# First group's attention in one fixed instruction order, with its value sums and key copies on GpSimd

## The chip, the cores and the metric

The kernel runs on one core of a Trainium2 chip. The metric is the device time of one execution in microseconds (us). A core has five engines that run their own instruction streams and wait for each other by semaphores: TensorE (PE in the profile; PEld is its weight loading), VectorE (DVE), ScalarE (ACT), GpSimd (POOL) and SyncE (SP), which here issues most of the DMAs.

## What is computed

Three layers run one behind the other on 8 x 576 = 4608 tokens of width 512, all in float32:

```python
# attention: q, k, v are (8, 8, 576, 64); keys and values averaged over 8 neighbours
k_p = k.reshape(B, H, Sp, pool, D).mean(axis=3)          # Sp = 72
v_p = v.reshape(B, H, Sp, pool, D).mean(axis=3)
attn = softmax(scale * q @ k_p.T);  x = attn @ v_p       # -> (4608, 512)
# first MLP: w_in (512, 2048), w_out (2048, 512)
h = x @ w_in;  g = max(h, 0) + log1p(exp(-abs(h)));  x = g @ w_out
# second layer: tokens with x @ w_skip > 0 go to the best of 8 experts (512 -> 1024 -> 512)
out = x + gate * (relu(x @ w1[e]) @ w2[e])               # other tokens: out = x
```

## The kernel before

Tokens are worked off in nine groups of 512 (G). For each group the attention makes x for four head pairs; a head pair with its tokens is a **unit**, and x is kept in two parts, `xh` (rounded to the matmul's own float32 format) and `xl` (the rest). The first MLP then goes through 16 chunks c of 128 hidden columns: `p1(g, c)` is 12 matmuls of 512 columns into `h` (L716), a softplus of four ScalarE and two VectorE instructions (Abs L722, Exp L723, Ln L724, the sum L725, the rounded part `gh` L727, the rest `gl` L729), and `p2(g, c)`, two chunks later, is 12 matmuls into four banks `y` (L740 to L742). p1 of a chunk reads the first half of that chunk's weight tile, and p2 of chunk c reads the second half of tile c + 2.

The weights arrive as raw words and are converted on the way, during group 0: two ScalarE instructions on the raw words (`unpack`, L470 and L472), two on VectorE (`join`, L475 and L477), the rounded part `wh` on ScalarE (L492 or L520) and the rest `wl` on VectorE (L494 or L521). `load_weights` is a generator with one such step per `next`; chunks 0 to 3 (`EARLY`) go by halves of 512 elements (L470 to L494, `half`), chunks 4 to 15 by pairs of 2 x 1024 (L520, L521).

Group 0's units (`unit0`) pool the keys on VectorE (`kp`, L531), copy them into a block-diagonal tile `kbd` on ScalarE (L538, L539), make the scores `s` on TensorE (L586), the maximum and the subtraction on VectorE (L594, L595), the exponential on ScalarE (L543), its sum, an addition and the reciprocal on VectorE (L544 to L546) and the multiplication on GpSimd (L547). The values are summed over 8 neighbours and turned in one go by 8 matmuls with the identity (L604), the shares are turned by transposes (`tr`, L613) and copied by ScalarE (`et`, L614), and two pairs of matmuls make the output `o` (L570), from which come `xh` (ScalarE, L572) and `xl` (VectorE, L573). Units of later groups (`unit`) sum their values on VectorE (L554).

Each engine's order is made when the program is built, by a scheduler that goes by priorities (program order, and 250 places ahead for group 0's softplus); instructions of the first units, of the conversions and of group 1's first units are therefore interleaved. SyncE issues the loads in the order in which the code asks for them; three raw buffers serve the six early halves.

Of the kernel before, what the change touches and what calls it, by code (L numbers as in the profile page):

```python
# [9 lines left out]
F32 = mybir.dt.float32  # L10
# [10 lines left out]
P = 128  # L21
# [4 lines left out]
SP = 72  # L26
# [10 lines left out]
def tile_kernel(ctx, tc, qT, kT, vT, wbits, w9, w1, w2, out):  # L37
# [383 lines left out]
    with ExitStack() as ph:  # L421
# [37 lines left out]
        STEPS = 6 * EARLY + 6 * (8 - EARLY // 2)  # L459
# [4 lines left out]
        def load_weights():  # L464
# [15 lines left out]
            def half(c, j, first):  # L480
# [8 lines left out]
                unpack(lo, hi)  # L489
# [10 lines left out]
            for c in range(EARLY):  # L500
                for j in range(2 if c >= LAG else 1):
                    yield from half(c, j, True)
            for i in range(EARLY // 2, 8):
# [5 lines left out]
                for j in range(2):  # L509
                    lo, hi = raw[:, j, :, 0], raw[:, j, :, 1]  # L510
                    unpack(lo, hi)
# [15 lines left out]
        count = [0]  # L527
        def keys(u, k, kv):
            if u not in pooled:
                kp = pp.tile([P, SP], F32, tag="kp", name="kp")  # L530
                nc.vector.tensor_reduce(kp, k.rearrange("p (s w) -> p s w", w=8), AX.X, ALU.add)  # L531
                v = kv()
                nc.sync.dma_start(out=v, in_=vT[u])
                pooled[u] = (kp, v, None)
# [15 lines left out]
        def sums(us, vr):  # L550
            for u, *_ in us:
                kp, v, vp = pooled[u]
                if vp is None:
                    nc.vector.tensor_reduce(vr, v.rearrange("p (s w) -> p s w", w=8), AX.X, ALU.add)  # L554
# [11 lines left out]
        def output(us, et, hp, xh, xl, ps=ps_a, tag="pa"):  # L566
            o = ps.tile([P, 512], F32, tag=tag, name="o")
# [4 lines left out]
            nc.scalar.activation(out=xh[:, hp, :], in_=o, func=AF.Copy, scale=0.125)  # L572
            nc.vector.scalar_tensor_tensor(out=xl[:, hp, :], in0=o, scalar=0.125,  # L573
                                           in1=xh[:, hp, :].bitcast(F32), op0=ALU.mult, op1=ALU.subtract)

        def unit0(hp, us, xh, xl, g):
            (u, r0, rn, c0), = us
            q, k = room("q", G, True), room("kv", 576, True)
            nc.sync.dma_start(out=k, in_=kT[u])
            nc.sync.dma_start(out=q, in_=qT[u, :, r0:r0 + rn])  # L580
            yield
            yield
            banks = [ps_y.tile([P, 512], F32, tag=f"y{hp % 2 * 2 + i}", name="s") for i in range(2)]
            kb = keys(u, k, lambda: room("kv", 576, True))
            for t in range(T):
                nc.tensor.matmul(banks[t // 3][:, t % 3 * 144:(t % 3 + 1) * 144],  # L586
                                 lhsT=q[:, t * P:(t + 1) * P], rhs=kb, start=True, stop=True)
            e = k.rearrange("p (a k) -> p a k", k=SP)
            st = room("st", 24, True)
            mx, sm, rc = (st[:, i * 8:(i + 1) * 8] for i in range(3))  # L590
            for b, (i, j) in enumerate(((0, 3), (3, 4))):
                s3 = banks[b][:, :(j - i) * 144].rearrange("p (a k) -> p a k", k=SP)
                m = mx[:, 2 * i:2 * j]
                nc.vector.tensor_reduce(m, s3, AX.X, ALU.max)  # L594
                nc.vector.tensor_tensor(out=e[:, 2 * i:2 * j], in0=s3, op=ALU.subtract,  # L595
                                        in1=m.unsqueeze(2).to_broadcast([P, 2 * (j - i), SP]))
            shares(e, sm, rc)
            yield
            yield
            kp, v, _ = pooled[u]  # L600
            v8 = v.rearrange("p (s w) -> p w s", w=8)
            pv = ps_h.tile([P, 512], F32, tag="h", name="pv")
            for w in range(8):
                nc.tensor.matmul(pv[:SP, :P], lhsT=v8[:, w], rhs=ident, start=w == 0, stop=w == 7)  # L604
            vp = pp.tile([SP, P], F32, tag="vp", name="vp")
# [411 lines left out]
```

## Time and profile before

| | us |
|---|---|
| median of 3 runs | 1362.04 (1360.51 to 1363.50) |
| the profiled execution, device time | 1360.56 |
| its span on the core | 1358.8 |
| TensorE busy in the span | 1330.1 (98%) |
| VectorE, ScalarE, GpSimd busy | 847.6, 595.0, 308.0 |

The profiled execution is 1.5 us under the median of the runs, and 1.8 us of it lie outside the span. TensorE is busy almost throughout, so the time is what TensorE has to do plus the places where it has to wait. In the 40 slices of the page (34 us each) the first slice has TensorE at six tenths; ScalarE and VectorE are at nine tenths in the two slices behind it and fall to five and seven tenths afterwards. [...]

### The profile page before, as it was taken

The numbers are of one execution on the slowest core, as the hardware profiler recorded it, in microseconds if no ns is written. First come the engines' busy times: TensorE is split into PE (matmuls) and PEld (weight loads), VectorE is DVE, ScalarE is ACT, GpSimd is POOL, SyncE is SP. The second block draws the span as 40 slices with busy tenths as digits, with TensorE's granted clock in tenths as the row PEclk, the third lists the DMA queues.
The fourth block names the chain that finished last, engine by engine and source line by source line (L and its number), as shares of the span: only waits on it lengthen the run. The fifth ranks groups of instructions, "written<-read, shape, count | busy, mean of one in ns | idle before, by whom it ended". The sixth has DMA issues, their size and how long they took to land. (4 is left out here: it accounts for less than half of the span.)

```text
span 1358.8 us, 21365 instructions
## 1 busy us (share of the span) xinstructions
PE 1330.1 (98%) x7030; PEld 1110.0 (82%) x7030; DVE 847.6 (62%) x1951; ACT 595.0 (44%) x1076; POOL 308.0 (23%) x375
## 2 busy tenths in 40 slices
PE   6999999999999999999999999999999999999996
PEld 5777787778878778778778778889989898989885
DVE  7998794974974964965946847545655332326263
ACT  6996544544555445545455444551111111114152
POOL 2010111121021030030130120343233343233334
PEclk9999999999999999999999999999999999999998
DMA  7642432241341340431421301503322222243363
GB/s 274 256 150 79 125 106 68 77 126 35 83 128 29 99 125 17 119 102 31 119 70 28 111 14 46 196 23 94 96 79 95 71 63 75 69 136 112 123 212 88
DMA packets 149743, 134.17 MB, mean 99 GB/s; under 512 B 100933, under 2 KB 116933, under 8 KB 147056
## 3 DMA queue, kind: packets, MB, share of 16 engines
q1 hardware_dynamic: 131744, 95.51, 24.3%
q0 software_dynamic: 17872, 37.13, 8.6%
q8 instruction: 60, 0.98, 0.3%
q14 instruction: 67, 0.55, 0.1%
HBM read 168.77 MB, written 29.67 MB: 146 GB/s over the span
## 5 line engine op out<-in xcount | busy, mean ns | idle before, releaser
L716 PE MATMUL h<-xh,wt 128*128 128x512 f32 x1152 | 379.7, 390 | 0.3 <-DVE xl L573 0.3
L716 PEld LDWEIGHTS h<-xh,wt 128*128 128x128 f32 x1152 | 216.2, 188 | 46.0 <-DVE xl L573 1.2
L740 PE MATMUL y<-wt,gh 128*128 128x512 f32 x576 | 232.8, 404 | 0.0
L894 PE MATMUL h<-xt,w1h 128*128 128x256 f32 x1280 | 226.4, 281 | 2.7 <-PEq L918 2.0
L120 DVE CUSTOM_DVE_ANT_0 junk<-rows,w9b 128x512 bf16<-128x512 f32 x324 | 222.4, 686 | 8.1 <-ACT rows L114 3.2
L741 PE MATMUL y<-wt,gh 128*128 128x512 f32 x576 | 225.2, 391 | 0.0
L742 PE MATMUL y<-wt,gl 128*128 128x512 f32 x576 | 225.1, 391 | 0.0
L716 PE MATMUL h<-xl,wt 128*128 128x512 f32 x576 | 224.7, 390 | 0.0
L894 PEld LDWEIGHTS h<-xt,w1h 128*128 128x128 f32 x1280 | 196.4, 188 | 5.1 <-issue 2.8
L894 PE MATMUL h<-xt,w1l 128*128 128x256 f32 x640 | 179.5, 280 | 0.7 <-DVEq L962 0.7
L898 ACT ACTIVATE hs<-h 128x512 fp32r<-128x512 f32 x80 | 47.7, 598 | 301.5 <-PE h L894 180.3
L722 ACT ACTIVATE a<-h 128x512 f32<-128x512 f32 x144 | 85.8, 596 | 175.8 <-PE h L716 169.7
L725 DVE SCALAR_TENSOR_TENSOR a<-h,a 128x512 f32<-128x512 f32 x144 | 98.5, 684 | 102.8 <-ACT a L724 102.2
L727 ACT ACTIVATE gh<-a 128x512 fp32r<-128x512 f32 x144 | 90.8, 631 | 160.6 <-DVE a L725 158.2
L740 PEld LDWEIGHTS y<-wt,gh 128*128 128x128 f32 x576 | 108.1, 188 | 35.2 <-ACT a L722 7.7
L742 PEld LDWEIGHTS y<-wt,gl 128*128 128x128 f32 x576 | 108.2, 188 | 25.5 <-issue 2.1
L716 PEld LDWEIGHTS h<-xl,wt 128*128 128x128 f32 x576 | 108.2, 188 | 22.3 <-issue 0.2
L741 PEld LDWEIGHTS y<-wt,gh 128*128 128x128 f32 x576 | 108.3, 188 | 20.0 <-issue 0.2
L729 DVE TENSOR_TENSOR gl<-a,gh 128x512 fp32r<-128x512 f32 x144 | 101.0, 701 | 37.6 <-ACT gh L727 34.9
L894 PEld LDWEIGHTS h<-xt,w1l 128*128 128x128 f32 x640 | 122.1, 191 | 0.9 <-DVEq L962 0.9
L928 DVE SCALAR_TENSOR_TENSOR ys<-y,xg 128x512 f32<-128x512 f32 x38 | 28.5, 750 | 145.3 <-PE y L926 115.8
L926 PE MATMUL y<-w2h,hs 128*128 128x512 f32 x304 | 118.5, 390 | 0.6 <-DVE hs L899 0.6
(198 smaller groups left out, 1815.0 us busy)
## 6 DMA issues: line engine op xcount, KB each, us to landing
w9b<-w SPq DMA_DIRECT2D x81, 256.0 KB
raw<-wbits SPq DMA_DIRECT2D x12, 1024.0 KB
x2d<-rows SPq DMA_DIRECT2D x36, 260.0 KB
et<-q SPq DMA_DIRECT2D x256, 32.0 KB
kv<-vT SPq DMA_DIRECT2D x28, 288.0 KB
kv<-kT SPq DMA_DIRECT2D x24, 288.0 KB
xm<-misc SPq DMA_DIRECT2D x160, 32.0 KB
misc<-misc SPq DMA_DIRECT2D x144, 32.0 KB
```

The costliest lines, as they stand in the source:

```text
L120: nc.vector.tensor_tensor_reduce(out=ws["junk"], in0=rows[t][:, :D], in1=w9b[e], scale=1.0, scalar=0.0, op0=ALU.mult, op1=ALU.add, accum_o ...
L716: nc.tensor.matmul(h, lhsT=l, rhs=r[:, kk, :], start=n == 0, stop=n == 11)
L722: nc.scalar.activation(out=a, in_=h, func=AF.Abs)
L725: nc.vector.scalar_tensor_tensor(out=a, in0=h, scalar=0.0, in1=a, op0=ALU.max, op1=ALU.add)
L727: nc.scalar.activation(out=gh, in_=a, func=AF.Copy)
L729: nc.vector.tensor_tensor(out=gl, in0=a, in1=gh.bitcast(F32), op=ALU.subtract)
L740: nc.tensor.matmul(y, lhsT=th, rhs=wh, start=c == 0, stop=False)
L741: nc.tensor.matmul(y, lhsT=th, rhs=wl, start=False, stop=False)
L742: nc.tensor.matmul(y, lhsT=tl, rhs=wh, start=False, stop=c == 15)
L894: nc.tensor.matmul(h[:, f2, :], lhsT=l, rhs=r[:, kk, :], start=n == 0, stop=n == 11)
L898: nc.scalar.activation(out=hh[:, fs, :], in_=h, func=AF.Relu)
L926: nc.tensor.matmul(y, lhsT=hl[:, f, js], rhs=ws["w2h"][:, f, :], start=False, stop=f == 7)
```

## The change

Group 0's attention is written as methods of a class `Unit0`, and a function `lead_in` calls them in one list. `in_order` then ties every instruction of an engine in that list to the one before it on the same engine, so the scheduler keeps the list's order on each engine; it may still put other instructions between.

- All four key, query and value loads are asked for first, then three raw weight halves; the later three halves follow, each two conversions ahead.
- A unit's pooled keys are copied to `kbd` by GpSimd instead of ScalarE.
- The values are summed by three GpSimd additions per unit (`add8`) and turned by one matmul, instead of 8 matmuls.
- Conversions of chunks 0 and 1 stand behind the units' exponentials. Conversions of chunks 2 and later wait for the last unit's `xh` on ScalarE, group 1's first pooling of a new batch for the last `xl` on VectorE, and the first two p1 blocks for the last transposes on TensorE (`issue_after`).

The core of the diff:

```diff
+                if first:
+                    yield
+                with after("ACT", first and c > 1):
+                    unpack(lo, hi)
...
-            for c in range(EARLY):
-                for j in range(2 if c >= LAG else 1):
-                    yield from half(c, j, True)
+            its = [half(c, j, True) for c in range(EARLY) for j in range(2 if c >= LAG else 1)]
+            for n in range(2):
+                next(its[n])
+                yield
+            for n, it in enumerate(its):
+                if n + 2 < len(its):
+                    next(its[n + 2])
+                yield from it
...
+        def add8(out, t):
+            t3 = t.rearrange("p (s w) -> p s w", w=8)
+            for n in (4, 2):
+                nc.gpsimd.tensor_tensor(out=t3[:, :, :n], in0=t3[:, :, :n], in1=t3[:, :, n:2 * n], op=ALU.add)
+            nc.gpsimd.tensor_tensor(out=out.unsqueeze(2), in0=t3[:, :, 0:1], in1=t3[:, :, 1:2], op=ALU.add)
...
+            def key(self):
...
+                nc.gpsimd.tensor_copy(self.kb[0:64, 0:SP], kp[0:64, :])
+                nc.gpsimd.tensor_copy(self.kb[64:128, SP:2 * SP], kp[64:128, :])
...
+            def vsum(self):
+                add8(self.vr, self.v)
...
+            with after("PE", g == 0 and c < 2):
...
-        feed.start(units_of(0), 1)
-        for i, it in enumerate(feed.units):
-            next(it)
-            if i:
-                weights(1)
-        while feed.units or jobs:
-            feed.tick()
+        def lead_in():
+            u0, u1, u2, u3 = us = units_of(0)
+            for u in us:
+                u.load_v()
+            weights(2)
+            u0.key()
+            u0.score()
+            u1.key()
+            u1.score()
+            u0.top()
+            u2.key()
+            u0.exp()
+            u0.share()
+            u2.score()
+            u0.vsum()
+            u1.top()
+            u1.exp()
+            u3.key()
+            u1.share()
+            u0.value()
+            u0.turned()
+            u3.score()
+            u2.top()
+            u2.exp()
+            u1.vsum()
+            u0.product()
+            u0.high()
+            u3.top()
+            u2.vsum()
+            u2.share()
+            u1.value()
+            u1.turned()
+            u3.exp()
+            u3.share()
             weights(1)
+            u1.product()
+            u1.high()
+            u3.vsum()
+            weights(1)
+            u0.low()
+            u1.low()
...
+        with in_order():
+            lead_in()
```

What stands where in the built programs, at three places. First GpSimd, behind the constants at the program's start. Before, four multiplications of group 0 (`boot_kv` holds keys, values and exponentials of group 0) are followed by group 1's (`q`):

```order
L88 CAST tok_i<-tok_f 128x36
L547 TENSOR_TENSOR boot_kv<-boot_kv,boot_171 128x576 x4
L649 MEMSET q 128x8x24
L547 TENSOR_TENSOR q<-q,st 128x8x72
L649 MEMSET q 128x8x24
```

and now, from the copies of the third unit's keys on:

```order
L637 COPY kbd_165<-kp 64x72
L638 COPY kbd_165<-kp 64x72
L662 TENSOR_TENSOR boot_kv<-boot_kv,boot_171 128x576
L612 TENSOR_TENSOR boot_kv<-boot_kv 128x72x4
L612 TENSOR_TENSOR boot_kv<-boot_kv 128x72x2
L613 TENSOR_TENSOR boot_171<-boot_kv 128x72
L637 COPY kbd_167<-kp 64x72
L638 COPY kbd_167<-kp 64x72
L662 TENSOR_TENSOR boot_kv<-boot_kv,boot_171 128x576
L612 TENSOR_TENSOR boot_kv<-boot_kv 128x72x4
L612 TENSOR_TENSOR boot_kv<-boot_kv 128x72x2
```

Copies and value sums have come between the multiplications (L662) of one unit and the next; on TensorE a unit's value matmul now stands ahead of its transposes.

Second, ScalarE at the program's start. Before, behind the first two units' key copies (`boot_171` are raw weight words, `boot_kv` an exponential):

```order
L470 ACTIVATE boot_171<-boot_171 128x512
L472 ACTIVATE boot_171<-boot_171 128x512
L543 ACTIVATE boot_kv<-boot_kv 128x576
L492 ACTIVATE wt_181<-boot_171 128x512
L470 ACTIVATE boot_171<-boot_171 128x512
L472 ACTIVATE boot_171<-boot_171 128x512
L543 ACTIVATE boot_kv<-boot_kv 128x576
```

and now, behind the table load:

```order
L655 ACTIVATE boot_kv<-boot_kv 128x576
L553 ACTIVATE kbd_165<-kp 64x72
L554 ACTIVATE kbd_165<-kp 64x72
L655 ACTIVATE boot_kv<-boot_kv 128x576
L579 ACTIVATE vp<-pv 72x128
L678 ACTIVATE boot<-tr 72x512 x2
L655 ACTIVATE boot_kv<-boot_kv 128x576
L589 ACTIVATE xh<-o 128x512
```

The exponentials (L655) have moved ahead of all conversions, and two key copies of group 1's first unit (L553, L554) have slipped in behind the first one.

Third, ScalarE ahead of the rounded weights of chunks 4 and 5 (L520 before, L529 now), in group 0's p1 blocks. Before, from the first Abs on (`raw_450` is the raw pair of chunks 4 and 5, `raw_516` of 6 and 7):

```order
L722 ACTIVATE a<-h 128x512
L472 ACTIVATE raw_450<-raw_450 128x1024
L723 ACTIVATE a<-a 128x512
L538 ACTIVATE kbd_167<-kp 64x72
L724 ACTIVATE a<-a 128x512
L722 ACTIVATE a<-h 128x512
L539 ACTIVATE kbd_167<-kp 64x72
L723 ACTIVATE a<-a 128x512
L470 ACTIVATE raw_516<-raw_516 128x1024
L727 ACTIVATE gh<-a 128x512
L724 ACTIVATE a<-a 128x512
L520 ACTIVATE wt_511<-v 128x1024 x2
```

and now, the last twelve rows ahead of the same place (`raw_504` is the pair 4 and 5, `raw_581` the pair 6 and 7, L799 the fourth chunk's Abs):

```order
L558 ACTIVATE q<-q 128x8x72
L470 ACTIVATE raw_504<-raw_504 128x1024
L799 ACTIVATE a<-h 128x512
L495 ACTIVATE wt_190<-boot_171 128x512
L800 ACTIVATE a<-a 128x512
L472 ACTIVATE raw_504<-raw_504 128x1024
L801 ACTIVATE a<-a 128x512
L470 ACTIVATE raw_581<-raw_581 128x1024
L472 ACTIVATE raw_581<-raw_581 128x1024
L804 ACTIVATE gh<-a 128x512
L470 ACTIVATE raw_581<-raw_581 128x1024
L529 ACTIVATE wt_533<-v 128x1024 x2
```

The pair's rounding stood behind 11 instructions counted from the first Abs, in the second chunk's softplus; it now stands behind 35, in the fourth chunk's, with three of the next pair's four unpackings ahead of it. From the end of group 1 on, the order of all engines is as it was.

## Rows read from the trace of the kernel before

**Rows 1.** Busy time by stage; columns: stage, length, engines' busy time, clock, DMA share, GB/s.

```profile
0.00:35.40 35.40, 24.32 (x146) 19.97 (x146) 26.12 (x55) 23.71 (x48) 8.36 (x45) 1.00 0.81 281
35.40:74.75 39.35, 37.56 (x171) 29.23 (x172) 37.35 (x49) 39.20 (x60) 2.48 (x3) 1.00 0.65 247
74.75:120.00 45.25, 45.04 (x205) 33.53 (x204) 42.51 (x57) 36.28 (x60) 4.45 (x4) 1.00 0.33 100
```

**Rows 2.** Timeline, TensorE: start, duration, line, tile; idle time before and its releaser.

```profile
35.41 0.50 PE L716 MATMUL h<-xh,wt 128*128 128x512 f32 x1 [0.32 <-DVE xl L573]
...
42.40 1.39 PE L636 MATMUL s<-kbd,q 128*64 128x144 f32 x8 [1.22 <-ACT kbd L539]
...
54.52 0.39 PE L716 MATMUL h<-xh,wt 128*128 128x512 f32 x1
...
66.20 0.39 PE L716 MATMUL h<-xh,wt 128*128 128x512 f32 x1
...
74.75 0.39 PE L716 MATMUL h<-xh,wt 128*128 128x512 f32 x1
```

**Rows 3.** Timeline, VectorE: the rests of the weights of chunks 4 to 7.

```profile
49.27 1.22 DVE L521 TENSOR_TENSOR wt<-v,wt 128x1024 fp32r<-128x1024 f32 x1
...
60.84 2.34 DVE L521 TENSOR_TENSOR wt<-v,wt 128x1024 fp32r<-128x1024 f32 x2
```

**Rows 4.** Timeline, TensorE, group 0's attention.

```profile
5.22 2.29 PE L586 MATMUL s<-kbd,boot 128*128 128x144 f32 x8 [5.22 <-ACT kbd L539]
...
16.61 2.81 PE L604 MATMUL pv<-ident,boot_kv 128*72 128x128 f32 x16
19.25 1.15 PE L586 MATMUL s<-kbd,boot 128*128 128x144 f32 x8
...
31.91 1.07 PE L613 MATMUL tr<-ident,boot_kv 128*72 128x128 f32 x8
32.91 1.08 PE L570 MATMUL o<-boot,vp 72*64 72x512 f32 x4
```

**Rows 5.** Timeline, ScalarE, group 0's attention and the early halves.

```profile
4.62 0.26 ACT L538 ACTIVATE kbd<-kp 64x72 f32<-64x72 f32 x1 [2.54 <-DVE kp L531]
...
9.66 0.66 ACT L470 ACTIVATE boot<-boot 128x512 f32<-128x512 f32 x1 [2.05 <-DMA boot<-wbits]
10.22 0.64 ACT L472 ACTIVATE boot<-boot 128x512 int32<-128x512 uint32 x1
...
28.41 1.09 ACT L614 ACTIVATE boot<-tr 72x512 f32<-72x512 f32 x2
```

**Rows 6.** Timeline, VectorE, group 0's attention: maxima, and the sum of an exponential.

```profile
7.07 0.82 DVE L594 TENSOR_REDUCE boot<-s 128x6 f32<-128x432 f32 x2
...
11.49 0.75 DVE L544 TENSOR_REDUCE boot<-boot_kv 128x8 f32<-128x576 f32 x1
```

**Rows 7.** Timeline, GpSimd: a multiplication of group 0 and one of group 1.

```profile
18.32 1.15 POOL L547 TENSOR_TENSOR boot_kv<-boot_kv,boot 128x576 f32<-128x576 f32 x1 [3.06 <-DVE boot L546]
...
51.61 1.97 POOL L547 TENSOR_TENSOR q<-q,st 128x576 f32<-128x576 f32 x1 [7.49 <-ACT a L724]
```

**Rows 8.** VectorE's early rests: all six (min/median/max), and the longest on the timeline.

```profile
L494 DVE TENSOR_TENSOR wt<-boot,wt x6: 687/692/1399, 13.6 to 38.9; 128x512 fp32r<-128x512 f32 x6
...
18.61 1.40 DVE L494 TENSOR_TENSOR wt<-boot,wt 128x512 fp32r<-128x512 f32 x1 [0.43 <-ACT wt L492]
```

**Rows 9.** Timeline, ScalarE in group 0's p1 blocks: first Abs, rounding of 4 and 5, prices.

```profile
38.73 0.63 ACT L722 ACTIVATE a<-h 128x512 f32<-128x512 f32 x1
...
45.00 1.99 ACT L520 ACTIVATE wt<-v 128x1024 fp32r<-128x1024 f32 x2
...
53.62 0.62 ACT L723 ACTIVATE a<-a 128x512 f32<-128x512 f32 x1
54.15 1.14 ACT L470 ACTIVATE raw<-raw 128x1024 f32<-128x1024 f32 x1
55.18 0.62 ACT L724 ACTIVATE a<-a 128x512 f32<-128x512 f32 x1
```

More of the change, by code (lines that the diff above doesn't have):

```diff
@@ L1 @@
 import math
-from contextlib import ExitStack
+from contextlib import ExitStack, contextmanager, nullcontext
 import concourse.bass as bass
@@ L510, in load_weights @@
                     lo, hi = raw[:, j, :, 0], raw[:, j, :, 1]
-                    unpack(lo, hi)
+                    with after("ACT", i < 4):
+                        unpack(lo, hi)
                     yield
@@ L527, in tile_kernel, with after @@
         count = [0]
+        behind = {}
+        def after(eng, cond=True):
+            return tc.issue_after(behind[eng]) if cond else nullcontext()
         def keys(u, k, kv):
@@ L530, in keys @@
                 kp = pp.tile([P, SP], F32, tag="kp", name="kp")
-                nc.vector.tensor_reduce(kp, k.rearrange("p (s w) -> p s w", w=8), AX.X, ALU.add)
+                with after("DVE", u == 4):
+                    nc.vector.tensor_reduce(kp, k.rearrange("p (s w) -> p s w", w=8), AX.X, ALU.add)
                 v = kv()
@@ new lines, in round_x, with rest_x, in_order @@
+        def round_x(o, hp, xh):
+            return nc.scalar.activation(out=xh[:, hp, :], in_=o, func=AF.Copy, scale=0.125)
+        def rest_x(o, hp, xh, xl):
+            return nc.vector.scalar_tensor_tensor(out=xl[:, hp, :], in0=o, scalar=0.125,
+                                                  in1=xh[:, hp, :].bitcast(F32), op0=ALU.mult, op1=ALU.subtract)
+        @contextmanager
+        def in_order():
+            traced = nc.cur_bb.bb.instructions
+            mark = traced[-1]
+            yield
+            start = next(k for k in reversed(range(len(traced))) if traced[k] is mark) + 1
+            prev = {}
+            for ins in traced[start:]:
+                if ins.engine in prev:
+                    tc.add_manual_dep(ins, prev[ins.engine].name,
+                                      mybir.DependencyInfo(mybir.DependencyClass.NoSync, mybir.DependencyReason.DATA),
+                                      reason="in_order")
+                prev[ins.engine] = ins
@@ L785, in last_group @@
                 split2()
-        feed.start(units_of(0), 1)
-        for i, it in enumerate(feed.units):
-            next(it)
-            if i:
-                weights(1)
-        while feed.units or jobs:
-            feed.tick()
-            weights(1)
+        def lead_in():
[32 more added lines that the diff above has]
+            u3.share()
+            weights(1)
+            u1.product()
[4 more added lines that the diff above has]
+            u1.low()
+            u2.value()
+            u2.turned()
+            weights(1)
+            u3.value()
+            u3.turned()
+            weights(1)
+            u2.product()
+            u2.high()
+            u2.low()
+            weights(1)
+            u3.product()
+            u3.high()
+            weights(1)
+            u3.low()
+        with in_order():
+            lead_in()
         pend = []
```

129 lines of the change are left out of this document (72 added, 57 removed).

## The prediction

> **What bounds the kernel now.** I read the busy time by stage first. Up to 35.4 us TensorE does group 0's attention; from 35.4 to 74.75 it is busy 37.56 of 39.35 us, from 74.75 to 120 45.04 of 45.25 [rows 1]. So time can be won in three places: the start of the first p1 matmul at 35.41, a 1.22 us wait at 42.40 and some 0.6 us of waits up to 74.75 [rows 1, 2]. The second reading is who is full beside it: from 35.4 to 74.75 ScalarE is busy 39.20 and VectorE 37.35 of 39.35 us [rows 1], with the softplus and the conversion of the weights. TensorE runs only just behind them. The rests of chunks 4 and 5 are done at 49.27 + 1.22 = 50.5 and wanted at 54.52; those of 6 and 7 at 60.84 + 2.34 = 63.2, wanted at 66.20 [rows 2, 3]: a stock of 4 and 3 us. ScalarE paid for it early: 23.71 us of work were done before 35.4 [rows 1], most of the six early halves among them (their rests run on VectorE from 13.6 on [rows 8]). An earlier start of p1 is therefore worth what this stock allows, less what the change takes out of it.
>
> **The change, part by part.** All times are estimates of one walk through the new orders, with the durations of the rows; a step on GpSimd gets 0.14 us to start behind another engine (the multiplication at 18.32 starts so behind a reciprocal [rows 7]).
>
> *Key copies on GpSimd.* ScalarE loses 8 copies of 0.26 [rows 5], 2.2 us with gaps. GpSimd shows no such copy; I take 0.25 each, ScalarE's price, and bound it by 0.1 and 0.5. Scores of the first unit start at 5.3, as before.
>
> *Value sums on GpSimd.* Removed are 64 matmuls of TensorE, 16 in 2.81 us [rows 4], some 9.5 us of work in which TensorE hid its other waits; they need no engine before them but the load. Added are 12 GpSimd additions over 288, 144 and 72 elements. The nearest row is the multiplication of 576 in 1.15 us, 1.97 beside VectorE [rows 7], so 0.6, 0.36 and 0.24 us, with handing over 1.6 us a unit (1.2 to 2.7).
>
> *The chain on GpSimd.* Unit 0's exponential starts at 9.5, no conversion being ahead of it; sum (0.75 [rows 6]), addition and reciprocal end at 11.4, multiplication at 12.8, sum of its values at 14.4. Its transposes stand behind the value matmul and go at 14.7, not 12.8. Unit 1's exponential stands on ScalarE behind group 1's two copies, which wait for unit 2's scores (10.8 + 2.29 [rows 4] = 13.1): 13.7; its reciprocal ends at 15.6, its multiplication at 17.0, the sums of values 1 and 2 at 20.2. Unit 2 is multiplied by 21.6. Unit 3's multiplication meets VectorE's joins, which read two operands: VectorE's rest of 0.69 took 1.40 in the one place where it met a multiplication (18.61 beside 18.32 [rows 7, 8]), and multiplications spread from 1.15 to 1.97. I add 0.6: 22.5 to 24.3. The last value sum ends at 25.9. [...]
>
> *From there to p1.* Value matmul, 8 transposes (1.07 [rows 4]), two copies (1.09 [rows 5]) and the last product (about 0.55) put the first p1 matmul at 28.4, 7.0 us earlier than 35.41. But the second early half has its unpack (2 x 0.56, the step from 9.66 to 10.22 [rows 5]) behind the last copies on ScalarE, its join behind that on VectorE (31.4), its rounding (32.1) ahead of the last `xh` (32.6), and `xl` ends at 33.4. So the 24 matmuls of chunks 0 and 1 wait 2.2 us inside and end at 36.4; before, at 42.40 - 1.22 = 41.2 [rows 2]. The lead is down to 4.8 us.
>
> *The arrears.* Now four early halves and all of chunks 4 and 5 remain for ScalarE; it has been idle some 19 us up to its first Abs at 35.1, before 35.4 it was idle 11.7 [rows 1]. Ahead of the rounding of chunk 4 stand 16 softplus steps of about 0.52 (53.62 to 54.15 [rows 9]), 9 half steps of 0.56, 7 unpacks of 1.03 (54.15 to 55.18), two copies and an exponential: 8.2 + 5.0 + 7.2 + 1.1 = 21.5 us, so 56.7, and 57.8 at its end. Before, this rounding started 6.3 us after the first Abs (45.00 against 38.73 [rows 9]). VectorE is as full: its rest of chunk 4 ends at 59.2. TensorE waits some 2.9 us for chunk 2, 0.4 for chunk 3, 2.1 for the second half of chunk 3's tile and 3.7 for chunk 4, which it starts at 57.8 against 54.52. Group 1's second unit, whose key copies stand behind one more unpack, holds it again until 61.7.
>
> *Sum.* From 61.7, 19 matmuls of 0.227 end chunk 4 and the second p2 at 66.0; 48 more and 1.2 us of group 1's products put p1 of chunk 7 at 78.1. Before it was 74.75 [rows 2], with one transpose of 0.23 less done. The loss is 78.1 - 74.75 - 0.23 = 3.1 us. Nothing gives it back: after 74.75 TensorE had 0.2 us of idle time in 45 [rows 1]. The later weights come up to 4 us later on VectorE and TensorE 3 us later, so the stock holds. The loads cost nothing: words that are needed at 21 were asked for behind twelve loads of 3.4 MB, 12 us at the 281 GB/s of [rows 1]; if that cover were gone, a late half would cost its delay.
>
> The profiled execution had 1360.56 us (1358.8 in the span), so the same execution would take 1363.7. It lay 1.5 below the median of 1362.04; with the median as base the forecast is **1365.1**.
>
> **The rivals.** About 0.2%, 2.7 us, is what a measurement of this kernel can tell from no change.
>
> (1) *The start's gain is kept.* If ScalarE's and VectorE's work ahead were not needed, TensorE would pay only the wait for chunk 2, starting it at 38.7 against 42.4 + 1.1: 1362.0 - 4.8 = 1357.2. It decides at the rounding of chunk 4: before 50 us this rival holds. For it speaks that stocks of 3 to 4 us exist [rows 2, 3], against it that ScalarE is busy 39.20 of 39.35 us there [rows 1] and that three of the next pair's four unpacks now stand ahead. Chance 0.12.
>
> (2) *A shorter start.* GpSimd additions at four fifths of my price take 1.0 us off, no clash with VectorE 0.6, a faster handing over 0.7; the whole of group 0 then moves forward with them, as all of it hangs on ScalarE's first Abs. All three give 1362.8, one or two 1363.5 to 1364.5: no change that can be told. Chance 0.35.
>
> (3) *TensorE slower in group 0's attention.* [...] Chance 0.13.
>
> (4) That the order isn't what the list says is excluded by the built program, save for what the scheduler slips between, which is in the walk.
>
> **How the numbers follow.** Forecast, 2.7 to about 6 us slower: 0.40, likeliest time 1365.1. With (3), slower has 0.53, (2) gives 0.35 to no change, (1) 0.12 to faster. The high end takes GpSimd's additions at 1.3 of my price (+1.5) and part of (3): 1369. The low end takes (2) and a little of (1): 1360.5. Left out are most of (1) and some 0.05 above.
>
> **What would show it.** Right: the first p1 matmul near 28, the last value sum on GpSimd near 26, ScalarE's first Abs near 35, the rounding of chunk 4 after 54, TensorE waits of over 8 us in all between 36 and 62, p1 of chunk 7 at 76 to 80. Wrong: a rounding of chunk 4 before 52; TensorE without waits for `wt` between chunks 1 and 5; or value sums that end before 22, which would bring everything forward by 4 us and more.

## The result, and the profile after

The changed kernel takes 1373.47 us (median of 6 runs, 1371.33 to 1377.0) against 1361.82 (6 runs, 1359.92 to 1363.5): ratio 1.0091, 95% interval 1.0074 to 1.0107, so 11.65 us slower. The forecast was 1365.1, 3.1 us slower, with 1369.0 as its upper end: right in sign, far too small. The profiled execution took 1375.84 us, its span 1374.1. All executions counted in this document are of one speed, save one of e8 below, which took 2704.1 us and is left out of its median.

By stage (length, busy time of TensorE, its weight loads, VectorE, ScalarE and GpSimd, granted clock, DMA share, GB/s), to be held against [rows 1]:

```profile
0.00:35.40 35.40, 23.71 (x90) 15.50 (x91) 20.27 (x44) 14.03 (x27) 16.73 (x65) 0.78 0.83 306
35.40:74.75 39.35, 31.76 (x121) 22.20 (x121) 34.19 (x50) 36.65 (x58) 2.49 (x3) 0.89 0.58 198
74.75:120.00 45.25, 45.14 (x210) 33.53 (x209) 43.98 (x59) 38.76 (x64) 4.98 (x5) 1.00 0.38 119
```

In the first stage ScalarE does 14.0 us of work where it did 23.7, and the granted clock reads 0.78 instead of 1.00. The trace has records of the clock only from its first change on, at 18.02 us in the kernel before and at 9.65 in the changed one, both to the upper level; a reading of 1.00 ahead of that says nothing (the last section shows the pace there). In the second TensorE is busy 5.8 us less, at 0.89. From 74.75 on it is full again. TensorE's timeline, to be held against [rows 2] and [rows 4]:

```profile
13.91 0.43 PE L577 MATMUL pv<-ident,boot 128*72 128x128 f32 x1 [2.40 <-POOL boot L613]
14.13 1.92 PE L676 MATMUL tr<-ident,boot_kv 128*72 128x128 f32 x8
...
28.56 0.30 PE L577 MATMUL pv<-ident,boot 128*72 128x128 f32 x1 [3.44 <-POOL boot L613]
28.70 1.04 PE L676 MATMUL tr<-ident,boot_kv 128*72 128x128 f32 x8
29.66 3.26 PE L585 MATMUL o<-boot,vp 72*64 72x512 f32 x8
32.85 0.80 PE L793 MATMUL h<-xh,wt 128*128 128x512 f32 x1
...
38.35 0.50 PE L793 MATMUL h<-xh,wt 128*128 128x512 f32 x1 [0.90 <-ACT wt L495]
...
43.99 0.50 PE L793 MATMUL h<-xh,wt 128*128 128x512 f32 x1 [1.84 <-ACT wt L495]
...
56.70 1.47 PE L817 MATMUL y<-wt,gh 128*128 128x512 f32 x4 [2.04 <-ACT wt L495]
...
63.96 0.55 PE L793 MATMUL h<-xh,wt 128*128 128x512 f32 x1 [2.65 <-ACT wt L529]
...
86.94 0.39 PE L793 MATMUL h<-xh,wt 128*128 128x512 f32 x1
```

The first p1 matmul comes at 32.85, 2.6 us earlier than before. It is followed by four waits for weights that ScalarE has not yet rounded, 7.4 us together. Chunk 4 starts at 63.96 (before 54.52) and chunk 7 at 86.94 (74.75). At the end of group 0 the kernel is 11 us behind, and 12 us from group 2 to the last chunk of the last group. The other 3.3 of the 15.3 us between the two spans lie behind the first MLP; the two profiled executions stand 2.4 us above and 1.3 us below the medians of their kernels. Eight transposes take 1.92 us at 14.13 and 1.04 at 28.70: half speed and full speed.

The granted clock in stretches of 5 us (same columns) shows the same; in the kernel before every such stretch from 18.02 up to 75 us is at 1.00:

```profile
10.00:15.00 5.00, 2.34 (x14) 1.98 (x15) 4.67 (x13) 1.48 (x4) 3.59 (x8) 0.81 1.04 404
15.00:20.00 5.00, 5.00 (x18) 3.01 (x17) 3.47 (x8) 1.82 (x4) 3.80 (x7) 0.50 1.05 410
...
30.00:35.00 5.00, 5.00 (x13) 2.43 (x10) 1.99 (x3) 2.05 (x4) 0.00 (x0) 0.51 0.84 292
35.00:40.00 5.00, 4.10 (x14) 2.52 (x14) 1.67 (x3) 2.51 (x6) 0.00 (x0) 0.80 0.01 2
...
55.00:60.00 5.00, 3.30 (x9) 2.65 (x10) 4.92 (x7) 5.00 (x8) 1.97 (x1) 0.74 0.73 267
```

0.50 is the lower of the two levels. In finer stretches the clock falls to it four times: at 13.1, inside the pause of 2.40 us that ends at 13.91; at 30.1, behind the pause of 3.44 us that ends at 28.56; and at 57.4 and 64.3, behind the waits of 2.04 and 2.65 us.

GpSimd's chain (compare [rows 7]) ends at 28.5, where the forecast had 25.9:

```profile
20.56 1.15 POOL L662 TENSOR_TENSOR boot_kv<-boot_kv,boot 128x576 f32<-128x576 f32 x1 [1.45 <-ACT xh L589]
24.50 1.49 POOL L662 TENSOR_TENSOR boot_kv<-boot_kv,boot 128x576 f32<-128x576 f32 x1 [2.79 <-ACT boot L472]
25.95 1.74 POOL L612 TENSOR_TENSOR boot<-boot 128x288 f32<-128x288 f32 x2
27.77 0.73 POOL L613 TENSOR_TENSOR boot<-boot 128x72 f32<-128x72 f32 x1
```

ScalarE, to be held against [rows 9], stands idle 5.4 us before a copy of group 1's keys, whose buffer is free only when TensorE has done group 1's first scores. Its first Abs starts at 40.56 and the rounding of chunks 4 and 5 at 62.87 (forecast 35.1 and 56.7):

```profile
37.49 0.26 ACT L553 ACTIVATE kbd<-kp 64x72 f32<-64x72 f32 x1 [5.44 <-PE s L708]
...
40.56 0.60 ACT L799 ACTIVATE a<-h 128x512 f32<-128x512 f32 x1
...
62.87 1.99 ACT L529 ACTIVATE wt<-v 128x1024 fp32r<-128x1024 f32 x2
```

**A balance.** From the first p1 matmul to about the 390th matmul of p1 and p2, added up from TensorE's timeline. "Slower" is what the intervals between these matmuls take over 0.227 us each, the step at full speed.

| kernel | first p1 | idle | slower | end | against before |
|---|---|---|---|---|---|
| before | 35.4 | 1.9 | 3.4 | 139.6 | |
| changed | 32.9 | 8.1 | 10.1 | 150.1 | +10.5 |
| e3 (below) | 30.1 | 8.3 | 8.0 | 146.0 | +6.4 |
| g1 (below) | 32.9 | 3.4 | 6.4 | 142.1 | +2.5 |

So the changed kernel wins 2.6 us at the start, waits 6.2 us more and runs its matmuls 6.7 us slower; 10.3 of the 10.5.

### The profile page after: what moved, and what is told of

It is laid out like the page before. It is cut to its first block, busy times and chain, and to the rows that moved or that the text cites. A ratio compares the mean times of both kernels' runs of the same rounds, so it can differ in the third digit from the quotient of the medians.

```text
span 1374.1 us, 21262 instructions
## 1 busy us (share of the span) xinstructions
PE 1333.8 (97%) x6970; PEld 1104.9 (80%) x6970; DVE 849.5 (62%) x1951; ACT 592.5 (43%) x1068; POOL 316.7 (23%) x395
## 5 line engine op out<-in xcount | busy, mean ns | idle before, releaser
L799 ACT ACTIVATE a<-h 128x512 f32<-128x512 f32 x144 | 85.8, 596 | 177.3 <-PE h L793 166.9
L817 PEld LDWEIGHTS y<-wt,gh 128*128 128x128 f32 x576 | 108.3, 188 | 37.3 <-ACT a L799 7.4
L819 PEld LDWEIGHTS y<-wt,gl 128*128 128x128 f32 x576 | 108.7, 189 | 23.7 <-issue 0.2
L1051 PE MATMUL y<-w2h,hs 128*128 128x512 f32 x304 | 118.5, 390 | 1.4 <-ACTq L1089 1.4
L1053 PE MATMUL y<-w2h,hs 128*128 128x512 f32 x304 | 118.5, 390 | 0.4 <-DVE hs L1026 0.4
```

Of the source, the lines that this page charges most:

```text
L799: nc.scalar.activation(out=a, in_=h, func=AF.Abs)
L817: nc.tensor.matmul(y, lhsT=th, rhs=wh, start=c == 0, stop=False)
L819: nc.tensor.matmul(y, lhsT=tl, rhs=wh, start=False, stop=c == 15)
L1051: nc.tensor.matmul(y, lhsT=hh[:, f, js], rhs=ws["w2h"][:, f, :], start=f == 0, stop=False)
L1053: nc.tensor.matmul(y, lhsT=hl[:, f, js], rhs=ws["w2h"][:, f, :], start=False, stop=f == 7)
```

## The experiments

Three theories. **A**, arrears: the conversions that the list puts behind the exponentials are missing later, and ScalarE's work sets when TensorE can go on. **C**, clock: TensorE's pauses put it to the lower level, and the slow matmuls are the loss beyond the forecast. **K**: group 1's key copy blocks ScalarE's queue. Later a fourth, **Q**: the value sums stand in GpSimd's queue ahead of the multiplications. All times are medians. The runs came in five batches, and each is set against the kernel before in its own batch (1361.25 to 1362.23); the intervals reach 1.2 to 2.2 us to either side.

| run | us | over before |
|---|---|---|
| changed kernel | 1373.5 | 11.7 |
| e1, e9: dummy matmuls | 1371.7, 1370.7 | 9.5, 9.4 |
| e2: group 1's copies later | 1371.7 | 9.5 |
| e3: values on TensorE | 1368.4 | 6.2 |
| e6: e3 and e2 | 1369.4 | 7.2 |
| e5: order not fixed | 1370.4 | 9.2 |
| e7, e8: conversions early | 1372.3, 1369.6 | 11.1, 8.4 |
| e12: more ScalarE work | 1376.9 | 14.6 |
| e11: conversions staggered | 1364.4 | 2.2 |
| g1, g2: outputs before p1 | 1363.1, 1364.6 | 1.4, 2.8 |
| f1, f2, f3: on top of e11 | 1372.2, 1366.9, 1372.4 | 10.2, 4.9, 10.4 |
| b1, b2, b2f: parts alone | 1364.3, 1365.9, 1365.4 | 2.0, 3.7, 3.4 |

### The clock: e1 and e9

In e1 this is called with n = 16 ahead of unit 0's value matmul and with n = 24 ahead of unit 3's:

```diff
+        def fill(ps, tag, n):
+            if n == 0:
+                return
+            pf = ps.tile([P, 512], F32, tag=tag, name="pf")
+            for _ in range(n):
+                nc.tensor.matmul(pf[:, :P], lhsT=ident, rhs=ident, start=True, stop=True)
```

e9 has, beside it, 6, 14 and 20 of these in p1 of group 0's chunks 1, 2 and 4, which p1's first matmul then overwrites:

```diff
+                for _ in range({1: 6, 2: 14, 4: 20}.get(c, 0) if g == 0 else 0):
+                    nc.tensor.matmul(h[:, :P], lhsT=ident, rhs=ident, start=True, stop=True)
```

> Two stretches in which TensorE stood idle in the changed kernel (2.4 us before the first value matmul, 3.4 us before the fourth) are filled with 16 and 24 matmuls of the identity whose results nobody reads; everything else is in the changed kernel's order. Theory C (the pauses lower TensorE's granted clock, and the slow matmuls behind them are what made the loss larger than forecast): granted clock 0.95 or more from 10 to 35 us, the first p1 matmul at 31 us or earlier (32.9 in the changed kernel), chunk 4 at 60 us or earlier (64.0), time 1368 to 1370 (1373.5). Theory K (ScalarE's queue is what is late: the copy of group 1's keys waits there for TensorE) with the clock unimportant: the clock recovers or not, the time stays 1372 to 1375. Theory A (the conversions are late by their order alone, as the forecast had it): 1372 to 1375, chunk 4 within 1 us of 64.0.

> The dummy matmuls of the first run, and 6, 14 and 20 more ahead of p1 of chunks 1, 2 and 4, in the pauses in which TensorE waits for the rounded weights. Theory C: granted clock 0.95 or more in every 5 us window to 75 us but one, 2 to 4 us better than the run with the first dummies alone (1371.7): 1368 to 1370. Theory A: the clock rises but the roundings come no earlier, TensorE's waits only grow by what it no longer loses; within 1 us of 1371.7.

e1: 1371.74 us. TensorE's timeline with the last unit's dummies (`pf`), the end of GpSimd's last value sum, and two stretches of 5 us:

```profile
22.20 5.52 PE L620 MATMUL pf<-ident 128*128 128x128 f32 x48
27.88 0.28 PE L577 MATMUL pv<-ident,boot 128*72 128x128 f32 x1
...
30.84 0.50 PE L801 MATMUL h<-xh,wt 128*128 128x512 f32 x1
```

```profile
25.27 0.73 POOL L613 TENSOR_TENSOR boot<-boot 128x72 f32<-128x72 f32 x1
```

```profile
15.00:20.00 5.00, 4.74 (x34) 3.34 (x33) 3.79 (x10) 3.58 (x9) 3.75 (x7) 1.00 1.06 410
...
30.00:35.00 5.00, 4.10 (x19) 2.18 (x16) 2.54 (x4) 2.79 (x7) 0.00 (x0) 1.00 0.83 349
```

The clock came back to 1.00 up to 41 us and the first p1 came 2.0 us earlier, as C had it. The time improved by about 2 us, 1.7 short of C's 1368 to 1370: the four waits up to chunk 4 grew from 7.4 to 8.7 us, and chunk 4 came at 61.3. The dummies cost something themselves: the last unit's value matmul waits for them until 27.88, though GpSimd's sum is done at 26.00.

e9: 1370.69 us. Its stage of 39.35 us:

```profile
35.40:74.75 39.35, 38.17 (x208) 31.29 (x207) 37.02 (x51) 39.16 (x64) 2.49 (x3) 1.00 0.68 244
```

Clock 1.00 in every stretch to 75 us, "slower" down from 10.1 to 4.6 in the balance, idle 1.9. And against its own kernel before it is no better than e1 (9.4 and 9.5 us over), as A had it: 9.0 us of dummies stand where the waits stood, and ScalarE is full (39.16 of 39.35). With the clock wholly restored the kernel still loses 9.4 us. Here too the dummies overran (the first p1 comes at 32.45, 1.6 us later than in e1), so the 9.4 us are an upper bound for what is left without C, and e1's 2 us at the start a lower bound for what C is worth. As far as e9 tells, the slow matmuls between the chunks lie mostly in time in which TensorE would wait for ScalarE anyway.

### ScalarE's queue: e2

Group 1's first copies stand behind the last `xh`:

```diff
-            nc.scalar.activation(out=kb[0:64, 0:SP], in_=kp[0:64, :], func=AF.Copy)
-            nc.scalar.activation(out=kb[64:128, SP:2 * SP], in_=kp[64:128, :], func=AF.Copy)
+            with after("ACT", count[0] <= 8):
+                nc.scalar.activation(out=kb[0:64, 0:SP], in_=kp[0:64, :], func=AF.Copy)
+                nc.scalar.activation(out=kb[64:128, SP:2 * SP], in_=kp[64:128, :], func=AF.Copy)
```

> The copies of group 1's first keys on ScalarE stand behind the last rounding of x, so that no instruction of ScalarE waits for TensorE between the third and the fourth rounding. Theory K: the idle 5.4 us of ScalarE is gone, the first Abs starts at 37 us or so (40.6), the wait before chunk 4 ends at 60 to 61 us (64.0), time 1369 to 1371. Theory C: TensorE's p1 matmuls at half clock still set the end of chunks 0 and 1, chunk 4 within 1.5 us of 64.0, time 1372 to 1374. Theory A: as C.

1371.67 us, between the ranges of K and C. The idle 5.4 us of ScalarE went, the first Abs came at 34.7, the roundings of chunks 4 and 5 4.4 us earlier, and chunk 11 was only 5.8 us behind the kernel before. Then the gain was given back at chunk 12. ScalarE, then TensorE:

```profile
58.46 2.01 ACT L529 ACTIVATE wt<-v 128x1024 fp32r<-128x1024 f32 x2
```

```profile
115.58 0.50 PE L794 MATMUL h<-xh,wt 128*128 128x512 f32 x1 [1.22 <-ACT wt L529]
```

At chunk 12 the first Abs is 12.1 us behind, against 5.8 one chunk earlier, and TensorE waits for a late rounding; part of these 6 us is work that changed places, since it stands at 8.8 in group 1 and at 10.0 behind it. K alone is not the cause.

### The value sums: e3, e6, and b2 and b2f on the kernel before

e3 has the values by eight matmuls per unit, as before the change; e6 is e3 with e2's edit; b2 is the kernel before with `add8` and one value matmul in place of the eight; b2f is b2 with seven dummies of the identity ahead of that matmul. The edit of e3:

```diff
             def vsum(self):
-                add8(self.vr, self.v)
+                pass
...
             def value(self):
-                values(self.us, self.vr, *((ps_h, "h") if self.hp < 2 else (ps_y, f"y{self.hp - 2}")))
...
+                for w in range(8):
+                    nc.tensor.matmul(pv[:SP, :P], lhsT=v8[:, w], rhs=ident, start=w == 0, stop=w == 7)
...
```

> One part undone: the values are summed by 8 matmuls per unit on TensorE as before the change, GpSimd keeps only the copies of the keys and the multiplications. Theory C: the 2.4 and 3.4 us pauses before the value matmuls go, clock 0.95 or more to 35 us, first p1 at 28 to 30 us, chunk 4 at 58 to 60 us, time 1366 to 1369. Theory K: first p1 earlier too, but ScalarE's copy still waits for group 1's first scores, 1369 to 1371. Theory A: only the 2.6 us that GpSimd's sums ran over the forecast come back, 1370 to 1372.

> Values summed on TensorE as before the change, and group 1's first key copies behind the last rounding of x. Theory C: about the time of the run that only puts the values back (1366 to 1369), within 1 us of it. Theory K: 3 us or more better than that run, 1363 to 1366. Theory A: equal to that run, and 3 us or more over the kernel before (1365 or more), since the conversions are still behind the exponentials.

e3: 1368.37 us, 5.1 better than the changed kernel, in C's range and outside those of A and K. TensorE:

```profile
28.20 1.94 PE L585 MATMUL o<-boot,vp 72*64 72x512 f32 x8
30.07 0.50 PE L801 MATMUL h<-xh,wt 128*128 128x512 f32 x1
...
59.17 0.79 PE L801 MATMUL h<-xh,wt 128*128 128x512 f32 x1 [2.66 <-ACT wt L529]
```

The clock is 1.00 up to 50 us, the first Abs at 35.9, the rounding of chunk 4 at 58.1. e6: 1369.42, not better than e3, where K had 1363 to 1366; K falls. Which part of the value sums costs, the clock or GpSimd's own time, b2 and b2f tell:

> The kernel before with one part of the change alone: the values of the first group summed by three GpSimd additions per unit (1.6 us) and one matmul in place of eight matmuls; scheduler, loads and conversions as before. Theory C: TensorE's work there gets thinner, its clock falls below 1.0 before 35 us and the p1 matmuls behind it run at half speed for a while, 1364 to 1367. Theory A: the conversions are where they were, so within 1.5 us of 1361.8.

> The kernel before with the values summed on GpSimd (as in the run of that part alone, 1365.9 us), and ahead of each value matmul seven matmuls of the identity whose result is overwritten, so that TensorE has as many matmuls there as in the kernel before. If the loss of that run (3.7 us) is the granted clock behind thin work: clock 0.95 or more from 25 to 45 us (0.50 to 0.85 there), 1362 to 1363.5. If it is GpSimd's 1.6 us per unit on the way to the first p1: 1365 to 1367.

b2: 1365.89 us, in C's range. The same stretch of b2, then of b2f:

```profile
35.00:40.00 5.00, 5.00 (x12) 2.70 (x11) 2.67 (x5) 4.50 (x8) 0.00 (x0) 0.50 1.03 426
```

```profile
35.00:40.00 5.00, 4.76 (x21) 3.95 (x22) 4.08 (x7) 5.00 (x7) 0.00 (x0) 1.00 1.03 424
```

b2f: 1365.36, in the range set down for GpSimd's time. Clock restored up to 44 us, the first p1 2.05 us earlier (35.24 against 37.29), and the time the same: the loss of b2 is not the clock. GpSimd's timeline in b2 shows what else there is:

```profile
14.79 1.66 POOL L579 TENSOR_TENSOR boot_kv<-boot_kv 128x288 f32<-128x288 f32 x2
...
16.80 1.78 POOL L579 TENSOR_TENSOR boot_kv<-boot_kv 128x288 f32<-128x288 f32 x2
18.66 0.31 POOL L580 TENSOR_TENSOR boot<-boot_kv 128x72 f32<-128x72 f32 x1
18.93 1.73 POOL L579 TENSOR_TENSOR boot_kv<-boot_kv 128x288 f32<-128x288 f32 x2
20.74 0.32 POOL L580 TENSOR_TENSOR boot<-boot_kv 128x72 f32<-128x72 f32 x1
21.02 1.15 POOL L547 TENSOR_TENSOR boot_kv<-boot_kv,boot 128x576 f32<-128x576 f32 x1
```

The second unit's shares are multiplied at 21.02; before at 18.32 [rows 7]. Its reciprocal starts at 18.14, before at 17.98, but the sums of three units stand ahead of it in GpSimd's queue. That is Q: 2.7 us at the head of the attention chain. TensorE, which summed the values before, had the time for it. How the 2.7 us reach the time, b2f tells in part, since its first p1 is not later than before (35.41). ScalarE's busy time up to 35.4 us is 22.27 (the fourth of the busy times below), before 23.71 [rows 1], its first Abs starts at 39.59 (38.73), and TensorE then waits for group 1's key copies:

```profile
0.00:35.40 35.40, 24.97 (x147) 19.61 (x148) 25.07 (x55) 22.27 (x47) 15.58 (x57) 1.00 0.76 264
```

```profile
44.29 2.48 PE L644 MATMUL s<-kbd,q 128*64 128x144 f32 x8 [3.31 <-ACT kbd L539]
```

That wait was 1.22 us before [rows 2]. So here too the delay is paid as work that ScalarE has still to do; this step is read from the rows and not tested by itself.

### The conversions: e12, e7, e8, e5

e12 repeats a rounding:

```diff
-                nc.scalar.activation(out=wh, in_=lo.bitcast(F32), func=AF.Copy)
+                for _ in range(3 if first and c > 1 else 1):
+                    nc.scalar.activation(out=wh, in_=lo.bitcast(F32), func=AF.Copy)
```

e7 has `weights(1)` twelve times in the list, from behind `u1.exp()` on; e8 is e7 with e3's edit. e5 takes the fixed order away:

```diff
-        with in_order():
+        with nullcontext():
             lead_in()
```

> The changed kernel with each high-part rounding on ScalarE of the four halves of chunks 2 and 3 done three times over instead of once (same output written again): 8 more instructions of about 0.56 us, 4.5 us of ScalarE between the first Abs and the rounding of chunks 4 and 5, nothing else touched. Theory A (ScalarE's arrears set when chunks 2 to 4 can start): the roundings of chunks 4 and 5 start at 66 to 67.5 us (62.9 in the changed kernel), time 1376.5 to 1378.5 (1373.5). Theory C (the granted clock alone, ScalarE's work has room): within 1.5 us of 1373.5.

1376.86 us, 3.4 more than the changed kernel in the median, in A's range. From the first Abs to the rounding of chunk 4 it takes 25.1 us instead of 22.3, and TensorE's idle time, counted as in the balance, grows by 3.4 us. But the rounding starts at 64.49, not at 66 to 67.5, since the first Abs came 1.1 us earlier; at the last chunk of the last group the profiled execution is only 1.5 us further behind than the changed kernel's (13.5 and 12.0); and the intervals of the two kernels, 1.0074 to 1.0107 and 1.0087 to 1.0117, overlap. So e12 has A's sign, and its size is not shown.

> The changed kernel with its list altered in one way: the steps of the weight conversions stand between the attention's steps from the second exponential on, twelve in all (four halves), in place of six behind the fourth exponential (two halves); loads, sums on GpSimd and key copies on GpSimd stay. Theory A (the deferred conversions are paid for later: TensorE's idle 7.4 us before chunks 0 to 4 are all ended by ScalarE's roundings of weights): the idle of TensorE from the first p1 to chunk 5 falls from 7.4 us to 3 us or less, the first Abs of chunk 4 comes 5 us or more earlier (71.1 in the changed kernel), time 1364 to 1368 (1373.5). Theory C (TensorE's granted clock): the pauses before the value matmuls stay, so the low clock to 40 us stays, and the time is 1369 to 1373. Theory K (ScalarE's queue blocked by group 1's key copy): 1370 to 1373.

> Conversions early as in the run before, and the values summed on TensorE as before the change; loads first, the fixed order and GpSimd's key copies stay. Theory A: chunk 4's first Abs at 62 us or earlier, time 1358 to 1363, so no worse than the kernel before (1362). Theory C: the same gain as from the values alone (5 us), 1366 to 1369.

> The changed kernel without the dependencies that fix each engine's order inside the list; the list itself, the loads and GpSimd's part stay, and the scheduler then puts the first conversions ahead of the first unit's transposes on ScalarE and the p1 matmuls of chunk 0 closer together. Theory A: part of the deferred conversions comes forward, time 1367 to 1371. Theory C or K: the pauses of TensorE before the value matmuls stay, time 1372 to 1375.

e7 1372.32, in the ranges of C and K, and e8 1369.62: A's numbers missed both times. ScalarE's timeline in e8:

```profile
24.92 0.68 ACT L495 ACTIVATE wt<-boot 128x512 fp32r<-128x512 f32 x1 [2.13 <-DVE boot L477]
...
30.14 0.67 ACT L495 ACTIVATE wt<-boot 128x512 fp32r<-128x512 f32 x1 [2.36 <-DVE boot L477]
...
37.02 0.66 ACT L495 ACTIVATE wt<-boot 128x512 fp32r<-128x512 f32 x1 [2.08 <-DVE boot L477]
...
40.28 1.08 ACT L807 ACTIVATE a<-h 128x512 f32<-128x512 f32 x2
```

Each rounding follows its own unpack in the fixed order and waits two microseconds for VectorE's join of it, with the attention's steps queued behind. The first Abs slipped to 40.3 (e3: 35.9), and what was won on the arrears was lost at the start. e5, where the scheduler places the same steps, came to 1370.4, in A's range but with an interval that reaches the next one.

### Staggered: e11, then f1, f2, f3, g1, g2

e11 is e3 with ten steps early in the list and in another order, where U is an unpack, J a join with its rounding, L a rest, and the number the half: U0 U1 J0 L0 U2 J1 L1 U3 J2 L2. So that U2 and U3 can stand there, the halves of chunk 2 no longer wait for the last rounding of x. The order comes from this:

```diff
-            for n, it in enumerate(its):
-                if n + 2 < len(its):
-                    next(its[n + 2])
-                yield from it
+            next(its[2])
+            yield next(its[0])
+            for n, it in enumerate(its):
+                if n + 1 < len(its):
+                    yield next(its[n + 1])
+                yield next(it)
+                yield next(it)
+                if n + 3 < len(its):
+                    next(its[n + 3])
```

f1 is e11 with 20 dummies in p1 of chunks 2 and 4. f2 is e11 with `behind["ACT"]` set to the first Abs, and group 1's later copies behind it. f3 is both. g1 is e11 with `behind["PE"]` set to the last output matmul of the first group. g2 is g1 with f2's edits.

> Values summed on TensorE; the first ten conversion steps stand early in the list as in the run with early conversions, but staggered: ScalarE unpacks the next half before it rounds the one that VectorE has joined, so that it does not wait 2 us for VectorE each time. Theory A: first Abs at 36 us or earlier, chunk 4's roundings at 53 us or earlier (58.1 with the values on TensorE alone), time 1361 to 1365. Theory C: granted clock as in that run, same time as that run, 1367 to 1369.

1364.38 us: 4.0 better than e3, in A's range, though the first Abs (37.3) and chunk 4's rounding (56.8) came later than expected. Same loads, same GpSimd copies, the list's order fixed as before: only where and in which order the conversions stand differs. That carries A. The two profiled executions stand 2.5 us apart at the last chunk of the last group (3.7 and 6.2 us behind the kernel before), so the gain is 2.5 to 4 us.

> The kernel with staggered conversions (1364.4 us), and 20 dummy matmuls of the identity in front of p1 of chunks 2 and 4, where TensorE waits 3.0 and 2.9 us. If the clock behind these pauses is what is left: granted clock 0.95 or more in all windows to 75 us, 1 to 2.5 us faster, 1362 to 1363.5. If the waits alone set the pace: 1364 to 1365.5.

> The kernel with staggered conversions, and on ScalarE the first Abs ahead of the unpacking of chunk 4 and of group 1's second pair of key copies. If ScalarE's order there is what is left: first Abs at 36 us or earlier (37.3), chunk 2's p1 1 us or more earlier (40.7), 1362 to 1363.5. If the amount of deferred work is what is left: 1364 to 1365.5, since the unpacking of chunk 4 is then later by as much.

> The two edits of the last two runs together. If both the clock and ScalarE's order are left over: 1360 to 1362, the kernel before or a little better. If neither: 1364 to 1366.

f1 1372.15, f3 1372.42: my dummies took 10.7 us where e11 waited 5.9, so they delayed chunk 2 by 4.4 us and say nothing of the clock. f2 1366.86: worse than either range, so ScalarE's order at the first Abs is not what was left. TensorE in e11, then ScalarE:

```profile
30.13 0.50 PE L806 MATMUL h<-xh,wt 128*128 128x512 f32 x1
...
32.86 1.08 PE L590 MATMUL o<-boot,vp 72*64 72x512 f32 x4
```

```profile
34.01 0.60 ACT L594 ACTIVATE xh<-o 128x512 fp32r<-128x512 f32 x1 [1.85 <-PE o L590]
```

The last unit's product stands behind eleven p1 matmuls of chunk 0, and the last rounding of x waits for it.

> The kernel with staggered conversions (1364.4 us), with p1 of chunks 0 and 1 held on TensorE behind the last unit's output product instead of behind its last transposes. If that queue is what is left: the wait of the last rounding of x (1.9 us) goes, the first Abs starts at 35 us or earlier (37.3), 1361 to 1363. If the deferred work of ScalarE sets the pace all the same: the first Abs earlier, chunk 4's roundings where they are, 1364 to 1365.5.

> The run before, with the first Abs and group 1's second pair of key copies placed as in the run with the Abs first. If ScalarE's order there counts once the rounding of x no longer waits: 0.5 to 1.5 us better than the run before. If the amount of deferred work counts: the same as the run before or up to 2 us slower.

g1: 1363.13 us, ratio 1.0008 (0.9999 to 1.0017), not to be told from the kernel before; better than e11 by 0.8, within the uncertainty. It lies between its two ranges; chunk 4's rounding came at 52.3 (56.8 in e11), though the first Abs was still at 36.4. Its stage:

```profile
35.40:74.75 39.35, 36.84 (x163) 27.93 (x162) 36.83 (x48) 39.06 (x60) 2.48 (x3) 1.00 0.67 258
```

The first p1 comes at 32.90, 2.5 us earlier than before and at the same time as in the changed kernel, with TensorE busy 36.84 instead of 31.76 and the clock at 1.00 without a dummy. g2, 1364.56, adds nothing. No version beats the kernel before.

### The key copies: b1

The kernel before, with this for the copy of the upper half of a unit's keys and the same for the lower half; `count` is 1 to 4 in the first group:

```diff
-            nc.scalar.activation(out=kb[0:64, 0:SP], in_=kp[0:64, :], func=AF.Copy)
...
+            (nc.gpsimd.tensor_copy(kb[0:64, 0:SP], kp[0:64, :]) if count[0] <= 4 else
+             nc.scalar.activation(out=kb[0:64, 0:SP], in_=kp[0:64, :], func=AF.Copy))
...
```

> The kernel before with one part of the change alone: the eight copies of the first group's keys on GpSimd (0.24 us each) in place of ScalarE (0.26). All theories: little moves, since ScalarE's copies there wait for VectorE's sums and not the other way round; 1361 to 1364 (1361.8).

1364.25 us, 2.0 more, just above the range. The scheduler, given other engines, placed VectorE's key sum of the third unit ahead of the first unit's maxima, where it waits 3.87 us for its load, and the first p1 came at 37.9. Whether the copies themselves cost anything stays open.

## Why the prediction was wrong

The bound was read rightly: TensorE just ahead of a full ScalarE, a small stock of rounded weights, and a start whose gain is taken back. By its steps:

1. **Key copies:** 0.24 us each measured, 0.25 taken. Right.
2. **The chain on GpSimd:** end 28.5 instead of 25.9. A unit's additions took 1.6 us (1.30 + 0.31) where I had 1.2, and 1.7 with handing over against 1.6; the last unit's, beside VectorE, 2.55. The second-last multiplication ends at 21.7 as in the walk (21.6), the last starts at 24.50 instead of 22.5: its exponential stands on ScalarE behind the second unit's two copies, and those waited for transposes at half speed (1.91 us at 20.02).
3. **From there to p1:** 4.4 us instead of 2.5. The products ran at half speed (3.26 us for 8; 1.94 in e3). And eight stand there: by the list the third unit's product is behind the last unit's transposes, and my walk had only the last product, with 0.55. The half speed was rival 3, which I gave 0.13 and priced at 2.8 us, an estimate from the two paces of eight scores, 2.29 us at 5.22 and 1.15 at 19.25 [rows 4]; the clock's row did not speak against it, since it has no record ahead of 18.02. No run shows these 2.8 us, part of which stand in my high end; what the trace shows is eight transposes at both levels, 1.92 us at 14.13 and 1.04 at 28.70, and the products' 3.26 us against 1.94. The 1.3 on GpSimd's additions in the same sum was an estimate too; they took 1.34 times my price (1.61 us a unit against 1.2). Together with 2 the first p1 came at 32.85, not 28.4.
4. **The first Abs:** 5.5 us later than in the walk, 40.56 against 35.1: 4.45 from the late p1, the rest from half-speed matmuls ahead of group 1's first scores, for which ScalarE waited. The key copies' place was in my walk only for a later unit.
5. **The arrears:** from the first Abs to the rounding of chunk 4 I had 21.6 us; it took 22.3, and 22.2 in e3. Right, and the waits of TensorE up to chunk 4 were not too small either: 2.2 and 9.1 forecast, 7.4 measured (the sign that I had set down, over 8 us, was missed).
6. **The sum:** chunk 4 at 63.96 instead of 57.8 is points 4 and 5 together (5.5 + 0.7). From chunk 4 to chunk 7 the walk had 20.3 us, the trace 23.0: matmuls at half speed behind the wait, and scores that moved in between. So chunk 7 came 12.2 us late, against 3.35 in the walk. How these 2.7 us divide is not shown.

The failing step is thus the start (2 to 4), the chain on GpSimd and from there to the first Abs: 5.5 of the 8.6 us between forecast and result. I had taken the start's gain as 7.0 and the lead after chunks 0 and 1 as 4.8; e3, which has neither the sums on GpSimd nor the low clock up to 50 us, has its first Abs at 35.9 and its rounding at 58.1, close to the walk, and still loses 6.2. The other 3 us of the miss, which e3 keeps, lie behind that rounding.

What the change costs, by undoing: the value sums about 5 us (e3), the place and order of the conversions 2.5 to 4 (e11 against e3), the rest 1 to 2 and hardly above the uncertainty. Of the 5 us at least about 2 come by the clock (e1). That the sums on GpSimd also cost without it, 3.4 us, b2f shows on the kernel before. How e3's gain divides between the two in the changed kernel is not measured.

Rival 1 fell: the rounding of chunk 4 came at 62.87, not before 50. Rival 2 fell with point 2.

## What to carry to other kernels

Work taken out of a lead-in is a loan from the engine that is full behind it: ask what that engine does in the next stage before moving it. In the changed kernel ScalarE did 14.0 us of work up to 35.4 where it had done 23.7, and its rounding of chunk 4 came at 62.87 instead of 45.00 [rows 9]. In a fixed order, two dependent steps on one engine with another engine's step between need something else placed between them: brought forward back to back the conversions gained nothing (e8 1369.6 us against e3's 1368.4), staggered 2.5 to 4 us (e11). And an engine at half speed is not always a loss: from b2 to b2f the clock between 35 and 40 us went from 0.50 to 1.00, and the time only from 1365.9 to 1365.4 us.

## What the runs showed of the hardware

- The granted clock of a stretch counts time without a record as 1.00, and the records begin with the first change. Up to 35.40 it reads 1.00 in [rows 1], but ahead of 18.02 us the kernel before runs at the slower pace: eight scores take 2.29 us at 5.22 and 1.15 at 19.25 [rows 4], six transposes behind a pause of 5.10 us take 1.50 us, and eight take 1.04 later:

```profile
15.32 1.50 PE L613 MATMUL tr<-ident,boot_kv 128*72 128x128 f32 x6 [5.10 <-POOL boot_kv L547]
...
23.60 1.04 PE L613 MATMUL tr<-ident,boot_kv 128*72 128x128 f32 x8
```

  The clock's first record, to the upper level, is at 18.02, when TensorE has worked without a pause since 15.32, and every stretch up to 75 us is at 1.00. The changed kernel has its first at 9.65, behind 16 scores without a pause from 5.22 on, and falls at 13.1, inside the pause of 2.40 us.
- In the changed kernel GpSimd took longer from 24.5 to 28.5 us, where VectorE did joins and rests beside it: its multiplication 1.49 us, and 1.15 at 20.56 with VectorE idle; its pair of additions 1.74 in place of 1.30, and its last 0.73 in place of 0.31. VectorE's second join (L477) took 1.52 us at 25.02, and 0.69 at 33.41 with GpSimd idle. Not all of VectorE's work did this: the additions at 12.16 took their 1.30 beside its maxima, subtractions and sums.
- GpSimd copies 64 by 72 numbers in 0.24 us in the changed kernel, where ScalarE took 0.26 in the kernel before [rows 5].
